# A layer of linear attention and a gated GLU: its side tasks dealt anew over two stages, and the scratch of the wo splits moved to other slots

## The chip, the cores and the metric

The kernel runs on one core of a Trainium2 chip. Its time is the device time of one execution in microseconds (us). Below, PE is TensorE (matmuls), DVE is VectorE, ACT is ScalarE, POOL is GpSimd, and SP is SyncE, whose queue issues nearly all DMAs.

## What is computed

With x of 2048 tokens by 1024 features and xn = layernorm(x), all in fp32:

```python
# 32 heads of 32 features; q, k, v = split(xn @ wqkv)
phi(a) = concat(softmax(a @ w_phi), softmax(-(a @ w_phi)))
num = phi(q) @ (phi(k).T @ v)                # per head, over all tokens
den = phi(q) @ sum(phi(k)) + 1e-6
s   = (num / den) @ wo
g   = silu((sigmoid(xn @ w_gate) * (xn @ w_up)) @ w_down)   # inner width 3584
out = x + s * g
```

## The kernel before

**Products.** Every large product of 2x2 blocks is made of seven block products and sums of blocks in place of eight (Strassen's scheme in Winograd's form). The seven are named B11, T2, T3, B21, T1, T4 and B22; they need sums of the blocks of both operands, and their results are combined as they leave PSUM. Each fp32 operand block is split into a high and a low fp32r part (`split`, L126: a cast on ACT at L128, a subtraction on DVE at L129), and each block matmul is three matmuls, high by high, high by low, low by high (`mm3`, L133 to L135).

**Stages.** The tokens go in two chunks, c = 0 and 1. For each chunk there is a projection stage (V, then K, then Q, each with seven products of 4 x 4 `mm3` in the order B11, B21, T2, T3, T4, T1, B22) and a GLU stage (28 units, gate and up in turn, of seven products of four `mm3`, in the order B11, T2, B21, T3, T1, T4, B22). So a GLU stage has 196 products, numbered by `m` in the code. Then come the down product for both chunks, and last the attention's numerators with the product by wo. The list `ops` holds all projection and GLU products; one loop (L803 on) emits them, each followed by `prep()`, which fills eight weight slots (28 to 35) ahead. In the first GLU stage all seven weight operands of a unit are split on the spot and the four that are sums are also stored to `ws_d`; in the second these four are loaded from there (L372).

**Slots.** On-chip memory is cut into 55 slots of 128 x 1024 fp32, grouped in blocks: x0 to x6 (0 to 27, the x operands, four slots each), w (28 to 35), p (36 to 38), fa (39 to 42), fb (43 to 46) and fc (47 to 54). The profile names the block, not the slot.

**Side tasks.** Other work of the layer is cut into tasks, which `background` (L797) takes from a queue, one at a given product:

- k tasks (`k_task`, L447), one a token tile and half of the heads: load k and v, softmax features on DVE and ACT, a running sum, two splits into 36 to 38, and eight matmuls (`kv_products`, L470) that the next call of `background` emits. They use 52, 53 and 54 too. After each half come `kv_sum`, `kv_blocks` and `z_broadcast`, which use PSUM banks 4 to 7 and the same slots.
- x tasks (`x_fetch` and `x_turn`, L522 and L529): load a tile of chunk 1's tokens, norm it, turn it, and store its x operands to `xo_d`; slots 52 to 54.
- q tasks (`q_features`, L598): the features of q; slots 36 to 38 for the first chunk, 43 and 44 for the second.
- o tasks (`o_task`, L257): load four blocks of wo into slots 52 and 53, make four sums on POOL (L269 to L272), split all seven operands through 36 to 38 in turn, and store them to `wo_d`, which the last stage reads.
- wd tasks (`wd_sums`, L558): load four blocks of w_down, make four sums on POOL, and store them to `wd_d`, for the down product's T2 and later; slots 47 and 52 for the first `WD1` of the 14, slots 43 and 44 for the others.

`tc.issue_after(anchor)` around a task lets its instructions be placed only behind the anchor, the last evacuation on DVE. Within that, the framework orders each engine's queue by its own simulated timeline; a slot that is used again makes the later user wait.

**Who runs where, before.** Beside the first Q projection, the k tasks of five tiles (behind T2, T3, T4, T1 and B22). In the first GLU stage 41 places: behind T2 of each unit from the second on, and behind T4 in units 0 to 13, so two a unit up to unit 13 and one a unit from there. They take the other three k tasks, then x and q tasks in turn (16 of each), then the four o tasks. In the second chunk's projections, eight wd tasks and five k tasks; in the second GLU stage 47 tasks, one at every fourth product: k tasks, six wd tasks and 16 q tasks, merged by the share of each that is left.

**The end of the first GLU stage.** In its last unit `load_operand` (L207) brings the second chunk's x operands from `xo_d`, in halves: half 0 through slot 53, half 1 through slot 54, each split into the x slots as soon as the last product that reads those is done. The V projection of chunk 1 follows at once.

Of the kernel before, what the change touches and what calls it, by code (L numbers as in the profile page):

```python
# [29 lines left out]
Q, K, V = 0, 1, 2  # L30
# [14 lines left out]
B11, T2, T3, B21, T1, T4, B22 = range(7)  # L45
# [3 lines left out]
def hedgehog_glu_kernel(  # L49
# [55 lines left out]
    block("fb", 43, 4, F32)  # L105
    block("fc", 47, 8, F32)
    NW = 8
    WD1 = 8

    banks = [psum.tile([P, HB], F32, name=f"bank{i}") for i in range(8)]  # L110

# [3 lines left out]
    def halves(*ids):  # L115
        return [slots[i][:, a] for i in ids for a in range(2)]

    def run(i, n):

        name, k = where[i]  # L120
        return blocks[name][0][:, k:k + n]
# [4 lines left out]
    def split(o, src):  # L126

        nc.scalar.copy(o[0], src)  # L128
        return nc.vector.tensor_sub(o[1], src, o[0].bitcast(F32))  # L129
# [127 lines left out]
    def o_task(k):  # L257

        def keep(i, b):
            o = slots[o_r.next()]  # L260
            split((o[:, 0].bitcast(F32R), o[:, 1].bitcast(F32R)), b)
            nc.sync.dma_start(wo_d[i, k], o.bitcast(F32).rearrange("p a n -> p (a n)"))

        a11, a12, a21, a22 = bs = halves(52, 53)
        for b, (f, h) in zip(bs, ((0, 0), (0, 1), (1, 0), (1, 1))):
            nc.sync.dma_start(b, wo[(k + 4 * h) * P:(k + 4 * h + 1) * P, f * HB:(f + 1) * HB])
        for i, b in ((B11, a11), (B21, a12), (T4, a22)):
            keep(i, b)
        nc.gpsimd.tensor_add(a22, a21, a22)  # L269
        nc.gpsimd.tensor_sub(a21, a11, a21)  # L270
        nc.gpsimd.tensor_sub(a11, a22, a11)
        nc.gpsimd.tensor_sub(a12, a12, a11)  # L272
        for i, b in ((T2, a11), (T3, a21), (T1, a22), (B22, a12)):
            keep(i, b)
# [109 lines left out]
    last_evac = []  # L384
# [173 lines left out]
    def wd_sums(j, *at):  # L558
        b11, b12, b21, b22 = b = halves(*at)
        for b, i in ((b11, B11), (b12, None), (b21, B21), (b22, B22)):  # L560
            nc.sync.dma_start(b, wd_block(i, j))
        sub = nc.gpsimd.tensor_sub
        sub(b11, b12, b11)
        sub(b12, b22, b12)
        sub(b22, b22, b11)
        sub(b21, b21, b22)
        for i, b in ((T1, b11), (T3, b12), (T2, b22), (T4, b21)):
            nc.sync.dma_start(wd_d[i, j], b)
# [29 lines left out]
    def q_features(t, hb):  # L598

        r, a, e = qf[t // CTT].next()  # L600
        p, e = slots[r][:, a], whole(e)
        nc.sync.dma_start(p, qkv_d[Q, t, hb])
        r = features(f"q{t}{hb}", p, e, True)
        nc.sync.dma_start(r_d[t, hb], r)
        nc.sync.dma_start(e_d[t, hb], e)
# [175 lines left out]
    qs = [lambda t=t, hb=hb: q_features(t, hb) for t in range(TT) for hb in range(2)]  # L781
    wd = [lambda j=j: wd_sums(j, *((47, 52) if j < WD1 else (43, 44))) for j in range(NJ)]
    xs = []
# [4 lines left out]
    bg_proj0 = deque(ks[0][:CTT])  # L788
    bg_glu0 = deque([lambda: block("p", 36, 3, F32)])
    for n in range(16):  # L790
        bg_glu0.extend([xs[n], qs[n]])
    bg_glu0.extend([lambda k=k: o_task(k) for k in range(4)])
    bg_proj1 = deque(wd[:WD1])
    late_k = deque(ks[0][CTT:] + ks[1])
    bg_glu1 = deque()

    def background(anchor, tasks):  # L797
        kv_products()
        if tasks:
            with tc.issue_after(anchor):  # L800
                tasks.popleft()()

    for n, (kind, c, what, i) in enumerate(ops):  # L803
        ws = ready[n]
        if kind == "proj":
            for u in range(4):
                if i in opening:
                    pbank[u] = pmm.next()
                xo = run(XO[i], 4)
                us = slice(u * P, (u + 1) * P)  # L810
                for k in range(4):
                    mm3(pbank[u], (xo[:, k, 0, us], xo[:, k, 1, us]), pair(ws[k]),
                        i in opening and k == 0, k == 3, skip_group_check=True)
                step()
            flow["used"] += 4
            while prep():
                pass
            for u in range(4):
                proj_out(c, what, i, u, pbank[u])
            if c == 0 and what == Q and i == B21:  # L820
                block("p", 36, 3, F32R)
            if c == 0 and what == Q and i not in (B11, B21):
                background(last_evac[0], bg_proj0)
            if c and not (what == V and i in (B11, B21)):
                background(last_evac[0], bg_proj1 if bg_proj1 else late_k if what == Q and i not in (B11, B21) else ())
            continue

        j, s = what
        u = units.index((c, j, s))
        if (j, s, i) == (0, 0, 0):  # L830
            step(1000)
        if i in opening:
            gbank[i] = gmm.next()
        bank = gbank[{B21: B11, T4: T3, B22: T1}.get(i, i)]
        w = [h.rearrange("p (k m) -> p k m", m=P) for h in pair(ws[0])]
        xo = run(XO[i], 4)
        for k in range(4):
            mm3(bank, (w[0][:, k], w[1][:, k]), (xo[:, k, 0], xo[:, k, 1]),
                i in opening and k == 0, k == 3, skip_group_check=True)
        flow["used"] += 1  # L840
        while prep():
            pass
        last_unit = u == len(units) - 1
        if flow["item"] == len(items) and flow["made"] - flow["used"] < NW:
            hfree.append(ws[0])
            if last_unit and i == 0:
                wfree.extend(range(16, 20))
            while wfree and down_prep():
                pass
        if i == B11:  # L850
            u1, u2 = ur.next(), ur.next()
            if s == 0:
                gates = [gates_r.next() for _ in range(4)]
            nc.scalar.copy(u1, bank)
        elif i == T2:
            v = nc.vector.tensor_add(u1, u1, bank)
        elif i == T3:
            v = nc.vector.tensor_add(u2, u1, bank)  # L858
        else:
            q = {B21: 0, T1: 3, T4: 2, B22: 1}[i]  # L860
            g = gates[q]
            if s == 0:
                if q == 0:
                    nc.scalar.activation(g, bank, AF.Sigmoid)
                else:
                    v = nc.vector.tensor_add(g, u2 if q == 3 else u1, bank)
                    nc.scalar.activation(g, g, AF.Sigmoid)
            else:
                if q == 0:
                    nc.vector.tensor_mul(g, g, bank)  # L870
                else:
                    b = u1 if q == 1 else u2
                    v = nc.vector.tensor_add(b, u2 if q == 3 else u1, bank)  # L873
                    nc.gpsimd.tensor_mul(g, g, b)  # L874
                if q != 1:
                    nc.sync.dma_start(h_d[(B11, None, B21, T4)[q], j, :, c], g)
                else:

                    a11, a21, a12, a22 = gates
                    s3, s2, s4 = [hs_r.next() for _ in range(3)]  # L880
                    nc.gpsimd.tensor_sub(s3, a11, a21)
                    nc.gpsimd.tensor_add(a21, a21, a22)
                    nc.gpsimd.tensor_sub(s2, a21, a11)
                    nc.gpsimd.tensor_sub(s4, a12, s2)
                    for o, b in ((T3, s3), (T1, a21), (T2, s2), (B22, s4)):
                        nc.sync.dma_start(h_d[o, j, :, c], b)

        m = (u % (2 * NJ)) * 7 + glu_order.index(i)
        if c == 0:
            if i == T2 and m > 7 or i == T4 and u < 14:  # L890
                background(v.ins, bg_proj0 or bg_glu0)
        else:
            if m == 0:
                rest = [deque(a) for a in (late_k, wd[WD1:], qs[16:])]
                total = [len(a) for a in rest]
                while any(rest):
                    q = max(range(3), key=lambda q: len(rest[q]) / total[q])
                    bg_glu1.append(rest[q].popleft())
            if m and m % 4 == 0:
                background(v.ins, bg_glu1)  # L900
        if c == 0 and u % (2 * NJ) == 2 * NJ - 1:
            if i == B11:
                load_operand(B11)
            elif i == B21:
                load_operand(B21)
            elif i == B22:
                for o in order[2:]:
                    load_operand(o)
                block("p", 36, 3, F32R)
# [114 lines left out]
    for tp_ in range(NTP):  # L1024
        nxt = attend(tp_ + 1) if tp_ + 1 < NTP else []
        n = 0
# [63 lines left out]
```

## Time and profile before

| | |
|---|---|
| median of 3 runs | 2440.74 us (2434.90 to 2442.89) |
| the profiled execution | 2439.86 us, its span 2438.0 us |
| granted TensorE clock, mean | 0.991 |
| moved by DMA | 626.17 MB, mean 257 GB/s |
| first GLU stage | from 302.5 to 866.7 us of the span |
| second GLU stage | from 1118.7 to about 1672 us |
| down product | from about 1672 us |

The profile is of one execution. A row of groups has: line, engine, operation, what it writes and reads with shapes, count | busy us, mean ns of one | idle time of the engine before it, and what ended that. A row of waits has: who waited for whom, us in total, times, the longest. A row of stretches has: the stretch, its length, then for each engine busy us and, in brackets, the number of instructions; then the granted clock, DMA's share and GB/s. A row of a timeline has: start, duration, engine, line, operation, and in square brackets the idle time before it and what ended it. A matmul's duration includes its way through the array, so the pace of TensorE is read from start to start.

### The profile page before, as it was taken

What the parts mean: (1) busy time and instruction counts of PE and PEld (TensorE: products, weight loads), DVE (VectorE), ACT (ScalarE), POOL (GpSimd) and SP (SyncE); (2) the same over time, 40 slices, a digit from 0 to 9 for tenths busy, and PEclk for the clock granted to TensorE, in tenths of its full rate; (3) what the DMA queues carried; (4) which work ended last, traced back from release to release, by engine and by line L of the source; (5) the groups of instructions that cost most, each with busy time, mean ns of one, the idle gap of its engine ahead of it and who ended that gap; (6) DMA issues with size and microseconds to landing.
All of it is one profiled execution on the core that took longest, in us unless ns stands there. A gap on an engine that the chain in (4) does not pass through costs nothing.

```text
span 2438.0 us, 31721 instructions
## 1 busy us (share of the span) xinstructions
PE 2360.2 (97%) x10728; PEld 1951.7 (80%) x10728; DVE 1786.3 (73%) x2341; ACT 996.5 (41%) x1485; POOL 1006.2 (41%) x638
## 2 busy tenths in 40 slices
PE   6999998999999969999999999999999999999998
PEld 5888876888888858888887888888888888788887
DVE  7533798888777856459758888875778786667885
ACT  6432355545444433234434434444333333345442
POOL 4530154676667743201334332333333334422655
PEclk9999999999999989999999999999999999999999
DMA  7874457999878999747787778779668766878664
GB/s 274 270 260 164 158 199 243 334 324 317 289 262 304 360 327 345 246 154 254 248 285 255 240 257 284 247 247 362 217 210 267 245 212 224 279 243 285 214 212 156
DMA packets 262323, 626.17 MB, mean 257 GB/s; under 512 B 37904, under 2 KB 58384, under 8 KB 257552
## 3 DMA queue, kind: packets, MB, share of 16 engines
q1 hardware_dynamic: 262160, 624.15, 75.1%
q8 instruction: 84, 1.38, 0.2%
q14 instruction: 79, 0.65, 0.1%
HBM read 374.47 MB, written 249.56 MB: 256 GB/s over the span
## 4 chain that ended last, share of the span: by engine, by line
PE 68%; DVE 13%; DMA 8%; issue 5%; POOL 3%; ACT 2%; SPq 1%; POOLq 0%; DVEq 0%; ACTq 0%
PE bank L133 22%; PE bank L135 22%; PE bank L134 22%; DVE w L129 3%; DVE x L129 1%; DMA fa<-w_down 1%; DVE p L129 1%; PE bank L475 1%; DMA fc<-xo_d 1%; DVE fc L452 1%; DMA f_d<-fc 1%; DMA fc<-qkv_d 0%; POOL fb L874 0%; DVE fc L435 0%; DMA w<-ws_d 0%
## 5 line engine op out<-in xcount | busy, mean ns | idle before, releaser
L133 PE MATMUL bank<-x,w 128*128 128x512 f32 x2352 | 912.2, 391 | 19.3 <-DVE fc L858 5.1
L134 PE MATMUL bank<-x,w 128*128 128x512 f32 x2352 | 918.0, 390 | 0.1
L135 PE MATMUL bank<-x,w 128*128 128x512 f32 x2352 | 907.7, 390 | 1.0 <-DVE w L129 1.0
L129 DVE TENSOR_TENSOR w<-fa,w 128x512 fp32r<-128x512 f32 (+1 forms) x444 | 447.7, 1012 | 213.5 <-ACT w L128 208.6
L133 PEld LDWEIGHTS bank<-x,w 128*128 128x128 f32 x2352 | 442.7, 188 | 120.3 <-DVE fc L858 8.2
L128 ACT CAST w<-fa 128x512 fp32r<-128x512 f32 (+1 forms) x444 | 308.4, 698 | 532.7 <-PE bank L134 385.9
L135 PEld LDWEIGHTS bank<-x,w 128*128 128x128 f32 x2352 | 442.8, 188 | 93.4 <-DVE w L129 1.4
L134 PEld LDWEIGHTS bank<-x,w 128*128 128x128 f32 x2352 | 442.9, 188 | 91.4 <-DVE x L129 1.0
L133 PE MATMUL bank<-w,x 128*128 128x512 f32 x708 | 279.5, 396 | 22.2 <-ACT x L128 19.8
L135 PE MATMUL bank<-w,x 128*128 128x512 f32 x708 | 278.5, 395 | 5.2 <-DVE x L129 5.1
L134 PE MATMUL bank<-w,x 128*128 128x512 f32 x708 | 279.0, 394 | 0.0
L874 POOL TENSOR_TENSOR fb<-fb,fc 128x512 f32<-128x512 f32 x57 | 90.5, 1588 | 219.5 <-DVE fc L873 202.7
L133 PEld LDWEIGHTS bank<-w,x 128*128 128x128 f32 x708 | 134.6, 190 | 52.2 <-ACT x L128 21.5
L613 POOL TENSOR_TENSOR fc<-fc 128x1024 f32<-128x1024 f32 x32 | 81.4, 2543 | 229.3 <-DMA fc<-e_d 120.4
L135 PEld LDWEIGHTS bank<-w,x 128*128 128x128 f32 x708 | 134.5, 190 | 35.0 <-DVE x L129 7.2
L134 PEld LDWEIGHTS bank<-w,x 128*128 128x128 f32 x708 | 134.6, 190 | 26.7
L129 DVE TENSOR_TENSOR x<-fa,x 128x512 fp32r<-128x512 f32 x112 | 117.1, 1046 | 33.8 <-ACT x L128 33.8
L334 POOL TENSOR_TENSOR fb<-fa 128x512 f32<-128x512 f32 x28 | 40.7, 1455 | 224.1 <-DMA fa<-w_gu 134.6
L129 DVE TENSOR_TENSOR w<-fb,w 128x512 fp32r<-128x512 f32 (+1 forms) x114 | 116.2, 1020 | 14.7 <-ACT w L128 14.6
L128 ACT CAST p<-fc 128x512 fp32r<-128x512 f32 x100 | 74.9, 756 | 124.6 <-DVE fc L452 77.8
L129 DVE TENSOR_TENSOR p<-fc,p 128x512 fp32r<-128x512 f32 x100 | 112.0, 1127 | 16.8 <-ACT p L128 16.7
L128 ACT CAST w<-fb 128x512 fp32r<-128x512 f32 (+1 forms) x114 | 70.7, 623 | 85.1 <-PE bank L134 70.7
(239 smaller groups left out, 3188.6 us busy)
## 6 DMA issues: line engine op xcount, KB each, us to landing
ws_d<-w SPq DMA_DIRECT2D x112, 512.0 KB, 4.6
w<-ws_d SPq DMA_DIRECT2D x112, 512.0 KB, 5.1
fa<-w_gu SPq DMA_DIRECT2D x84, 512.0 KB, 4.9
fa<-h_d SPq DMA_DIRECT2D x84, 512.0 KB, 4.7
fa<-wf_d SPq DMA_DIRECT2D x32, 1024.0 KB, 6.4
h_d<-fc SPq DMA_DIRECT2D x120, 256.0 KB, 4.4
h_d<-fb SPq DMA_DIRECT2D x76, 256.0 KB, 4.8
fc<-qkv_d SPq DMA_DIRECT2D x64, 256.0 KB, 3.6
```

The source lines that it names most:

```text
L128: nc.scalar.copy(o[0], src)
L129: return nc.vector.tensor_sub(o[1], src, o[0].bitcast(F32))
L133: nc.tensor.matmul(o, a[0], b[0], start=first, stop=False, **kw)
L134: nc.tensor.matmul(o, a[0], b[1], start=False, stop=False, **kw)
L135: nc.tensor.matmul(o, a[1], b[0], start=False, stop=last, **kw)
L334: nc.gpsimd.tensor_add(s1, a21, a22)
L452: nc.vector.tensor_mul(e3, e3, r[:, :, None].to_broadcast([P, 32, DH]))
L475: nc.tensor.matmul(kvb[g // 2][:, g % 2 * 256:g % 2 * 256 + 256], v[:, g].rearrange("p a f -> p (a f)"), ph[:, g].rearrange("p a f -> p (a ...
L613: nc.gpsimd.tensor_mul(ez, e, zb)
L874: nc.gpsimd.tensor_mul(g, g, b)
```

## The change

The four o tasks leave the first GLU stage and are put at the head of the wd tasks in the second one; their four blocks are held in slots 43 and 44 instead of 52 and 53. `WD1` goes from 8 to 6, so two wd tasks more come in the second GLU stage. Beside the first Q projection four k tasks are started instead of five, behind B11, T2, T4 and B22. In the first GLU stage the four k tasks that are left, a change of the p block, four x tasks, then x and q tasks in turn, and four q tasks, 37 in all, are put at products 7 to 185 at even spacing. In the second, 53 tasks are put at products 3 to 187 at even spacing, where there were 47 at every fourth product.

```diff
--- before.py
+++ after.py
@@ -105,7 +105,7 @@
     block("fb", 43, 4, F32)
     block("fc", 47, 8, F32)
     NW = 8
-    WD1 = 8
+    WD1 = 6
 
     banks = [psum.tile([P, HB], F32, name=f"bank{i}") for i in range(8)]
 
@@ -261,7 +261,7 @@
             split((o[:, 0].bitcast(F32R), o[:, 1].bitcast(F32R)), b)
             nc.sync.dma_start(wo_d[i, k], o.bitcast(F32).rearrange("p a n -> p (a n)"))
 
-        a11, a12, a21, a22 = bs = halves(52, 53)
+        a11, a12, a21, a22 = bs = halves(43, 44)
         for b, (f, h) in zip(bs, ((0, 0), (0, 1), (1, 0), (1, 1))):
             nc.sync.dma_start(b, wo[(k + 4 * h) * P:(k + 4 * h + 1) * P, f * HB:(f + 1) * HB])
         for i, b in ((B11, a11), (B21, a12), (T4, a22)):
@@ -788,8 +788,9 @@
     bg_proj0 = deque(ks[0][:CTT])
     bg_glu0 = deque([lambda: block("p", 36, 3, F32)])
     for n in range(16):
-        bg_glu0.extend([xs[n], qs[n]])
-    bg_glu0.extend([lambda k=k: o_task(k) for k in range(4)])
+        bg_glu0.extend([xs[n]] if n < 4 else [xs[n], qs[n - 4]])
+    bg_glu0.extend(qs[12:16])
+    os = [lambda k=k: o_task(k) for k in range(4)]
     bg_proj1 = deque(wd[:WD1])
     late_k = deque(ks[0][CTT:] + ks[1])
     bg_glu1 = deque()
@@ -817,10 +818,10 @@
                 pass
             for u in range(4):
                 proj_out(c, what, i, u, pbank[u])
-            if c == 0 and what == Q and i == B21:
+            if c == 0 and what == Q and i == B11:
                 block("p", 36, 3, F32R)
-            if c == 0 and what == Q and i not in (B11, B21):
-                background(last_evac[0], bg_proj0)
+            if c == 0 and what == Q:
+                background(last_evac[0], bg_proj0 if i in (B11, T2, T4, B22) else ())
             if c and not (what == V and i in (B11, B21)):
                 background(last_evac[0], bg_proj1 if bg_proj1 else late_k if what == Q and i not in (B11, B21) else ())
             continue
@@ -887,16 +888,21 @@
 
         m = (u % (2 * NJ)) * 7 + glu_order.index(i)
         if c == 0:
-            if i == T2 and m > 7 or i == T4 and u < 14:
-                background(v.ins, bg_proj0 or bg_glu0)
+            if m == 0:
+                bg_glu0.extendleft(reversed(bg_proj0))
+                bg_proj0.clear()
+                due = [7 + n * 178 // (len(bg_glu0) - 1) for n in range(len(bg_glu0))]
+            if m in due:
+                background(v.ins, bg_glu0)
         else:
             if m == 0:
-                rest = [deque(a) for a in (late_k, wd[WD1:], qs[16:])]
+                rest = [deque(a) for a in (late_k, os + wd[WD1:], qs[16:])]
                 total = [len(a) for a in rest]
                 while any(rest):
                     q = max(range(3), key=lambda q: len(rest[q]) / total[q])
                     bg_glu1.append(rest[q].popleft())
-            if m and m % 4 == 0:
+                due = [3 + n * 188 // len(bg_glu1) for n in range(len(bg_glu1) + 1)]
+            if m in due:
                 background(v.ins, bg_glu1)
         if c == 0 and u % (2 * NJ) == 2 * NJ - 1:
             if i == B11:
```

## The prediction

> **What bounds the kernel now.** I read the page first, for the engine that sets the time.
>
> ```profile
> span 2438.0 us, 31721 instructions
> PE 2360.2 (97%) x10728; PEld 1951.7 (80%) x10728; DVE 1786.3 (73%) x2341; ACT 996.5 (41%) x1485; POOL 1006.2 (41%) x638
> ```
>
> TensorE is busy 97% of the span, so only its gaps can be won. Next I cut the span at the stages and asked for the busy time of each stretch.
>
> ```profile
> core 0: us, PE busy (x) PEld busy (x) DVE busy (x) ACT busy (x) POOL busy (x), PEclk, DMA share, GB/s
> 227.00:302.50 75.50, 75.50 (x343) 62.80 (x342) 48.75 (x60) 25.40 (x31) 7.99 (x5) 1.00 0.46 153
> 302.50:392.00 89.50, 81.10 (x354) 64.65 (x353) 84.39 (x100) 44.83 (x64) 39.64 (x22) 0.96 0.59 207
> 392.00:502.00 110.00, 104.81 (x450) 83.93 (x449) 97.99 (x141) 55.34 (x77) 70.22 (x48) 0.98 0.90 316
> 502.00:780.00 278.00, 277.05 (x1221) 228.54 (x1220) 220.64 (x307) 132.00 (x194) 178.40 (x120) 1.00 0.84 294
> 780.00:866.70 86.70, 86.70 (x383) 71.35 (x382) 76.86 (x75) 36.56 (x61) 62.11 (x40) 1.00 0.98 359
> 866.70:910.00 43.30, 24.25 (x97) 18.95 (x96) 18.53 (x17) 16.17 (x22) 20.63 (x14) 0.80 0.92 315
> 1118.70:1257.00 138.30, 138.30 (x637) 115.35 (x636) 106.17 (x144) 62.10 (x85) 45.32 (x32) 1.00 0.81 276
> 1257.00:1396.00 139.00, 135.21 (x607) 112.06 (x607) 106.82 (x139) 57.02 (x76) 42.07 (x27) 0.99 0.74 244
> 1396.00:1672.00 276.00, 274.57 (x1254) 228.18 (x1253) 228.45 (x284) 120.36 (x163) 93.88 (x63) 1.00 0.78 267
> 1672.00:1800.00 128.00, 128.00 (x567) 106.01 (x566) 87.96 (x118) 46.13 (x81) 46.59 (x22) 1.00 0.75 256
> ```
>
> The first row is the last 75 us of the Q projection of chunk 0; 302.5 to 866.7 is the first GLU stage, 866.7 begins the second chunk's projections, 1118.7 to 1672 is the second GLU stage. The undisturbed pace is 277.05/1221 = 0.227 us a matmul, so a product of 12 takes 2.72 us. What each stretch loses against that pace, slow clock included: 302.5 to 392 has 354 matmuls, 48 of them the narrow ones of six k tasks (8 each, counted half, an estimate): 306 x 0.227 + 48 x 0.113 = 74.9, so 14.6 us lost. 392 to 502: 450 x 0.227 = 102.2, 7.8 lost. 502 to 780: 1.0. 780 to 866.7: nothing. 866.7 to 910: 97 x 0.227 = 22.0, 21.3 lost. Second GLU stage, by idle time: 0 + 3.8 + 1.4 = 5.2. That is 49.9 us in all that this change can reach.
>
> The largest loss is one gap, which the timeline of TensorE shows, then those of SyncE, GpSimd and ScalarE:
>
> ```profile
> 877.35 0.39 PE L135 MATMUL bank<-w,x 128*128 128x512 f32 x1
> 895.73 0.80 PE L133 MATMUL bank<-w,x 128*128 128x512 f32 x1 [17.99 <-ACT x L128]
> ```
> ```profile
> 861.33 0.44 SPq L266 DMA_DIRECT2D fc<-wo  x1
> ...
> 885.91 2.43 SPq L211 DMA_DIRECT2D fc<-xo_d  x2
> ```
> ```profile
> 881.22 1.27 POOL L272 TENSOR_TENSOR fc<-fc 128x512 f32<-128x512 f32 x1
> ```
> ```profile
> 894.63 1.04 ACT L128 CAST x<-fc 128x1024 fp32r<-128x1024 f32 x1 [6.45 <-DMA fc<-xo_d]
> ```
>
> Slots 52 and 53 hold the four blocks of an o task; load_operand stages half 0 of every x operand in 53. The last o task still loads wo at 861.33, its GpSimd sums end at 882.5, and only then, at 885.91, is x loaded into 53; its split begins when that lands at 894.6, and the product follows at 895.73. So the chain is slot 53, not bandwidth: the o task ahead of the load in the slot's order.
>
> The second loss is VectorE's. TensorE's waits inside the first GLU stage are led by an evacuation:
>
> ```profile
> PE bank L133 <- DVE fc L858: 5.1, 6, 2.3
> ```
>
> VectorE is busy 84.39 of 89.5 us there (94%), because six k tasks run in it, one every (390.4 - 305.4)/5 = 17 us:
>
> ```profile
> L463 DVE TENSOR_TENSOR fc<-fc x6: 1211/1212/1715, 305.4 to 390.4; 128x1024 f32<-128x1024 f32 x6
> ```
>
> **The change, part by part.** Prices of VectorE in the first GLU stage, first by operation, then all the work of a q task (tile stq) and most of a k task's (tile stk; this view names the first GLU stage, then the second):
>
> ```profile
> L129 DVE TENSOR_TENSOR w<-fb,w 128x512 fp32r<-128x512 f32 x110 | 110.3, 1003 | 14.7 <-ACT w L128 14.6
> L129 DVE TENSOR_TENSOR w<-fa,w 128x512 fp32r<-128x512 f32 x82 | 85.0, 1036 | 6.3 <-ACT w L128 6.3
> L129 DVE TENSOR_TENSOR p<-fc,p 128x512 fp32r<-128x512 f32 x28 | 31.7, 1146 | 6.1 <-ACT p L128 6.1
> L873 DVE TENSOR_TENSOR fc<-fc,bank 128x512 f32<-128x512 f32 x41 | 27.7, 676 | 16.4 <-PE bank L135 10.3 <-POOL fb L874 4.7 <-POOL fc L874 1.2
> ```
> ```profile
> 302.50:866.70 564.20, 87.89 (x96) 0.99 0.83 294
> ```
> ```profile
> 302.50:866.70 564.20, 32.13 (x35) 0.99 0.83 294
> 1118.70:1672.00 553.30, 126.59 (x145) 1.00 0.77 264
> ```
>
> The stage's own work: 7 splits a unit at 1.0 and 5.5 evacuations at 0.68, 10.7 us in 19.05 us, or 1.53 a product. A q task is 87.89/16 = 5.5 us. A k task is 126.59/20.7 = 6.1 (145 operations, 7 a task), plus zacc 1.2, the value split 1.15 and the wide split about 1.4 (twice a 0.68 operation): 9.9. An x task is 1.4 (four 0.68 operations for two tasks; the norm's one-column ones left out). An o task is 7 splits: 8.0.
>
> *k tasks earlier and fewer in Q.* Five in the last five Q products become four, one each second product. The Q stretch loses nothing today with VectorE at 48.75 of 75.5, and one task fewer is 9.9 less: no gain, no cost. Today six k tasks run beside the first GLU stage; after, the one behind B22 and four more at products 7, 11, 16, 21. One k task of 17 us meets 6.2 products of own work (9.6) and 9.9 of its own plus a wait on its exponential: over 17 either way, so beside k tasks VectorE stays too full. Five for six, the first with more room: 14.6 becomes 9.5 (between 3, if lag drains in the 4.9 products between tasks, and 15). **-5.**
>
> *x first, then x and q evenly.* 37 tasks at 178/36 = 4.94 products instead of two a unit up to unit 13. A pair then has 26.9 us for 15.1 + 5.5 + 1.4 = 22.0, 82%; today it has 19.05 for 10.7 + 6.9, 92%. The nearest rows: 220.64/278 (79%) lost 1.0 us, 76.86/86.7 (89%) nothing. So 7.8 becomes 0.8. **-7** (-4 to -8). The four q tasks left to the end have 13.4 us each for 7.6 + 5.5, 98%, where today nothing is lost: **+0.5** (0 to 5).
>
> *o tasks out of the first GLU stage.* Slot 53's last user before load_operand is then the last x turn, at product 160 of 196, some 98 us before the stage ends; both halves of B11 can wait in 53 and 54. What is late next is the following half through the two slots, for which the view of that line has the landing:
>
> ```profile
> DMA to landing us min/median/max: 4.8/5.8/8.7
> ```
>
> 5.8 us of load and some 3 of split (1.04 on ScalarE by the cast above, two 1.0 operations' worth on VectorE): about 9 us an operand with two slots, against 4 x 4 x 3 x 0.227 = 10.9 us a projection product, and B11 and B21 have their x slots free 7 and 5 products before the stage's end. It keeps pace. 21.3 becomes 2, for a short wait or two. **-19.3** (-10 to -21).
>
> *o tasks and two more wd tasks in the second GLU stage*, one task each 3.55 products instead of 4. The row of GpSimd for an o task:
>
> ```profile
> L269 POOL TENSOR_TENSOR fc<-fc x4: 1684/1792/2272, 779.4 to 875.1; 128x512 f32<-128x512 f32 x4
> ```
>
> The merge puts the four o tasks at products 6, 24, 38 and 52. VectorE gains 32 us and GpSimd 16 x 1.7 = 27, nearly all by 1280. Three of them bring the first 138 us to 106.17 + 24 = 130, 94%. Bounds: the 94% of 302.5 to 392 lost 14.6/89.5, or 16%, which is 22 us; the 89% of 780 to 866.7, with o tasks themselves in it, lost nothing. I take **+6**, nearer the latter: it is the same task. Two wd tasks move into the stage with no VectorE work; their 8 sums and 16 DMAs leave the second chunk's projections, for which I count no gain, and take 43 and 44: nothing, unless the slots jam, below. The o tasks' 44 DMAs pass SyncE's queue, and their 4 x (1.0 + 3.6) = 18.4 MB come to 114 GB/s over 161 us, less some 25 for two wd tasks that leave that part: 276 + 89 = 365 GB/s, where 359 is the most that a row above shows. What the products wait for is
>
> ```profile
> w<-ws_d SPq DMA_DIRECT2D x112, 512.0 KB, 5.1
> ```
>
> and eight w slots leave it 7 products or 19 us; 359 GB/s beside the first stage's own loads cost nothing. Taken at 0, inside the 6.
>
> Sum: -5 - 7 + 0.5 - 19.3 + 6 = -24.8. The profiled execution took 2439.86 (1.9 around its span), the median of the runs 0.9 more: 2440.7 - 24.8 = **2416**.
>
> **Two rules beside the rows.** After a short wait the clock is halved here:
>
> ```profile
> 367.99 0.79 PE L133 MATMUL bank<-x,w 128*128 128x512 f32 x1 [2.32 <-DVE fc L858]
> ...
> 369.01 0.63 PE L135 MATMUL bank<-x,w 128*128 128x512 f32 x1
> 369.44 0.63 PE L133 MATMUL bank<-x,w 128*128 128x512 f32 x1
> ```
>
> 0.43 us apart instead of 0.227, after 2.32 us of idling. The Trainium skill (TensorE: Matmul & The Clock Gate, Part 1: The HAM clock gate) has the clock fall only after an idle window of about 3.4 us; by that rule the k part's remaining waits would cost themselves alone, an estimate of 7 rather than 9.5, and the time would be some 2.5 us lower. I stay with the row.
>
> The other one speaks against the change. Splits of one shape differ by what runs beside them:
>
> ```profile
> L129 DVE TENSOR_TENSOR p<-fc,p x19: 679/1774/1784, 783.5 to 866.3; 128x512 fp32r<-128x512 f32 x19
> ```
> ```profile
> L129 DVE TENSOR_TENSOR w<-fa,w x22: 678/683/1779, 1120.4 to 1256.6; 128x512 fp32r<-128x512 f32 x22
> ```
>
> The median is 1.77 where GpSimd is busy 62.11 of 86.7 us and 0.68 where it is 45.32 of 138.3. The Trainium skill (GPSIMD Engine Reference, 1. Specifications) says that GpSimd's way to SBUF is shared with VectorE and contended by instructions with two SBUF inputs; the rows agree.
>
> **The rivals.** *VectorE fills up beside the o tasks (0.14).* By those rows 27 us of GpSimd stretch 27 x (1 - 0.68/1.77) = 17 us of VectorE work. Then the first 138 us are full, and lose the 16%: 22 for 6. Time 2432, near the line of no change; with the four late q tasks at their 5, 2436.
>
> *Part of the gap stays (0.18).* If the halves come through 53 and 54 more slowly than 10.9 us an operand, or the late q tasks hold back their splits, half the gap is left: +9, 2425. For it: one of these loads took 8.7 us, and DMA stands at 0.92 to 0.98 there. Against it: 9 us an operand is under 10.9, with both halves of the first waiting.
>
> *Slower: slots 36 to 38 jam (0.11).* An o task and a k task both need them.
>
> ```profile
> L262 SPq DMA_DIRECT2D wo_d<-p x28: 319/324/1732, 778.1 to 888.9; - x28
> ```
> ```profile
> L519 ACT COPY fc<-bank x4: 587/589/590, 1267.7 to 1681.1; 128x512 f32<-128x512 f32 x4
> ```
>
> Four o tasks held them from 778 to some 894, 29 us each. Up to product 56 the second GLU stage has 53 x 2.82 = 150 us for 4 x 29 + 4 k tasks x 17 = 184, 34 late; fifteen later k tasks come every 20.1 us and take 17, which regains 47. So they end in time, 13 us to spare. At 44 us an o task they end 47 late. z_broadcast, which now ends at 1681.7 without a loss (128.00 of 128.00), would hold the banks of the down products' second chunk until 1729: 45 us of waiting, 2440.7 - 31 + 6 + 45 = 2461. The point is an o task of about 40 us. Against it: a k task needs these slots only for its last operations. Slots 43 and 44, which q, wd and o tasks share, will run late as well, but what comes of them is wanted late: the first wd sums only at T2, 14 steps of 24 matmuls or 76 us into the down product.
>
> **How the numbers follow.** Forecast 0.57 (2403 to 2424); part of the gap 0.18; full VectorE 0.14, of which 0.10 within 0.3%; jam 0.11. 0.3% is 7.3 us, about what a measurement of this kernel can tell from no change. Faster 0.79, same 0.10, slower 0.11. The low end takes the k part's 3, the gap's -21 and nothing in the second GLU stage: 2440.7 - 11.6 - 8 - 21 = 2400. The high end is the full VectorE with late q tasks, 2437; above it lies the jam.
>
> **What would show it.** Right: no TensorE wait over 3 us between 850 and 910; L211's first two loads 90 us ahead of the stage's end; L858 waits fewer after 392; wo_d stores from 1130 to 1300, with VectorE over 85% there. Wrong: a gap after the second GLU stage with L519 later than 1690, or PE idle over 15 us between 1100 and 1260.

## The result, and the profile after

The changed kernel takes 2423.14 us (median of 5 runs, 2418.18 to 2425.68), the kernel before 2440.69 us beside it (5 runs). The ratio is 0.993, 95% interval 0.9909 to 0.995: about 17 us or 0.7% faster. The profiled execution of after is the slowest of its five, 2425.68 us with a span of 2423.9, 14.1 us under the span of before. All stretches below are of that execution, and its stages come earlier as it goes on: the first GLU stage ends at 854.7 us (866.7 before), the second begins at 1084.4 (1118.7).

The stretches of the kernel after, up to the start of the second chunk's projections, with the columns of the prediction:

```profile
302.50:392.00 89.50, 85.40 (x380) 70.44 (x379) 84.79 (x101) 42.95 (x61) 43.91 (x25) 0.96 0.62 228
392.00:502.00 110.00, 108.13 (x473) 88.86 (x472) 81.80 (x117) 50.20 (x74) 68.42 (x48) 0.98 0.86 286
502.00:780.00 278.00, 276.88 (x1222) 228.93 (x1221) 217.70 (x304) 130.27 (x187) 177.80 (x123) 1.00 0.82 287
780.00:854.70 74.70, 74.70 (x332) 61.84 (x331) 59.28 (x76) 33.77 (x48) 33.56 (x23) 1.00 0.75 273
854.70:910.00 55.30, 55.30 (x246) 45.79 (x245) 37.45 (x33) 25.46 (x29) 27.07 (x18) 1.00 0.94 332
```

The last row is the place of the 18 us gap: TensorE is busy 55.30 of 55.30 us at full clock. From 302.5 to 392 it now does 380 matmuls where it did 354, from 392 to 502 it does 473 instead of 450. VectorE's share from 392 to 502 has gone from 89% to 74%.

The second GLU stage went the other way. A good ruler for it is the copy that opens each of its 28 units (line 854 before, 855 after): the time from the first to the last of them is 27 units. The rows of that line, before and then after:

```profile
L854 ACT COPY fc<-bank x28: 562/580/590, 1121.6 to 1670.6; 128x512 f32<-128x512 f32 x28
```
```profile
L855 ACT COPY fc<-bank x28: 565/581/590, 1087.3 to 1658.6; 128x512 f32<-128x512 f32 x28
```

549.0 us before, 571.3 after: 22.3 us lost. By the same ruler the first GLU stage went from 543.7 us (307.5 to 851.2) to 535.4 (307.0 to 842.4). The whole second stage, before and then after:

```profile
1118.70:1685.00 566.30, 561.09 (x2553) 466.33 (x2552) 448.97 (x578) 244.45 (x330) 184.28 (x123) 1.00 0.78 267
```
```profile
1084.40:1671.80 587.40, 567.86 (x2553) 467.30 (x2551) 468.73 (x605) 259.40 (x358) 223.28 (x147) 0.99 0.85 296
```

The first row ends at 1685, where the last product of the stage is done; the prediction had taken its end at 1672. The same 2553 matmuls take 21.1 us more: TensorE's idle time went from 5.2 to 19.5 us, and its busy time grew by 6.8 us at a clock of 0.99 instead of 1.00. VectorE's share is 79% before and 80% after, so its sum of work over the stage does not explain the loss. The longest groups of TensorE's waits are these:

```profile
PE bank L133 <- DVE fc L859: 4.5, 3, 3.1
PE bank L475 <- DVE p L129: 4.1, 2, 3.3
PE bank L133 <- DVE fb L867: 3.6, 3, 2.8
PE bank L133 <- ACT fc L855: 3.1, 3, 2.5
```

They are few and long, and 13 of the 19.5 us are behind VectorE: it was not short of time on average, but late at some places.

### The profile page after: what moved, and what is told of

Read it like the earlier page. It is cut to its first block, busy times and chain, and to the rows that moved or that the text cites. A ratio compares the mean times of both kernels' runs of the same rounds, so it can differ in the third digit from the quotient of the medians.

```text
span 2423.9 us, 31722 instructions
## 1 busy us (share of the span) xinstructions
PE 2359.0 (97%) x10728; PEld 1952.8 (81%) x10728; DVE 1760.6 (73%) x2341; ACT 996.8 (41%) x1484; POOL 1001.3 (41%) x638
## 5 line engine op out<-in xcount | busy, mean ns | idle before, releaser
L129 DVE TENSOR_TENSOR w<-fa,w 128x512 fp32r<-128x512 f32 (+1 forms) x444 | 442.4, 1000 | 215.1 <-ACT w L128 197.1
L875 POOL TENSOR_TENSOR fb<-fb,fc 128x512 f32<-128x512 f32 x57 | 90.8, 1592 | 203.1 <-DVE fc L874 203.1
L875 POOL TENSOR_TENSOR fc<-fc 128x512 f32<-128x512 f32 x27 | 41.0, 1518 | 230.1 <-ACT w L128 172.4
L128 ACT CAST x<-fa 128x512 fp32r<-128x512 f32 x112 | 69.4, 620 | 75.7 <-DMA fa<-wd_d 38.9
```

## The experiments

Two theories stood at first for the second GLU stage: (A) the o tasks hold slots 36 to 38 and make the k tasks late; (B) the two wd tasks more, with their sums on GpSimd, and the denser dealing. Each kernel below was timed beside the kernel before on its own chip. "First copies" is the ruler above, of one profile each. The times of one kernel lie up to 10 us apart from run to run, and the profiled execution of after is the slowest of its five, so a difference of a few us between two rulers says little by itself.

**o_dma_only.** The o tasks of the changed kernel without their sums and splits:

```python
# the whole body of o_task
        for b, (f, h) in zip(halves(43, 44), ((0, 0), (0, 1), (1, 0), (1, 1))):
            nc.sync.dma_start(b, wo[(k + 4 * h) * P:(k + 4 * h + 1) * P, f * HB:(f + 1) * HB])
        for i in (B11, B21, T4, T2, T3, T1, B22):
            nc.sync.dma_start(wo_d[i, k], whole(43 + i % 2))
```

> The changed kernel, whose o tasks keep their 44 DMAs and their hold on slots 43 and 44 but leave out the sums and splits (raw blocks of wo are stored), so they no longer use slots 36 to 38, VectorE, ScalarE or GpSimd. In the changed kernel the first copies of the 28 units of the second GLU stage lie 571.3 us apart from first to last, before 549.0. Theory A (the o tasks' part on slots 36 to 38 and on VectorE makes the k tasks late, which then bunch and fill VectorE): that distance falls to 547 to 556 and the time to 2400 to 2409. Rival B (two more wd tasks, their sums on GpSimd, and the denser dealing, whatever the o tasks do): the distance stays at 564 or more, the time at 2416 or more.

```profile
L843 ACT COPY fc<-bank x28: 564/578/589, 1087.0 to 1646.8; 128x512 f32<-128x512 f32 x28
```

559.8 us; 2415.8 us, ratio 0.9907 (0.9886 to 0.9928). It falls between the two: 11.5 of the 22.3 us are gone with the o tasks' work, 10.8 stay without it. Neither theory holds alone.

**wd8.** The changed kernel with

```diff
-    WD1 = 6
+    WD1 = 8
```

> The changed kernel with WD1 back at 8: six wd tasks instead of eight in the second GLU stage, 51 tasks instead of 53. Theory A (o tasks make k tasks late): the distance of first copies in the second GLU stage stays within 5 us of 571.3 and the time at 2418 to 2427. Rival B (wd sums on GpSimd stretch VectorE's operations, and the dealing is too dense): a third or more of the 22 us comes back, distance 555 to 564, time 2405 to 2415.

```profile
L855 ACT COPY fc<-bank x28: 565/577/590, 1088.2 to 1644.6; 128x512 f32<-128x512 f32 x28
```

556.4 us, ratio 0.9887 (0.9869 to 0.9906), 2410.6 us. Two of 53 tasks account for 14.9 of the 22.3 us by the ruler, and for 12.6 us by the medians (10.5 by the ratios); both are inside what B expected. All four o tasks are still in the stage. The 11.5 us that go with the o tasks' work and the 14.9 that go with two wd tasks add up to more than 22.3, so the two parts make each other worse.

**o_only.** The kernel before with the o tasks alone moved:

```diff
-        a11, a12, a21, a22 = bs = halves(52, 53)
+        a11, a12, a21, a22 = bs = halves(43, 44)
...
-    bg_glu0.extend([lambda k=k: o_task(k) for k in range(4)])
+    os = [lambda k=k: o_task(k) for k in range(4)]
...
-                rest = [deque(a) for a in (late_k, wd[WD1:], qs[16:])]
+                rest = [deque(a) for a in (late_k, os + wd[WD1:], qs[16:])]
...
-            if m and m % 4 == 0:
+            if m in [3 + n * 188 // 51 for n in range(52)]:
```

> The kernel before with one part of the change alone: the four o tasks go from the first GLU stage to the head of the wd tasks of the second, in slots 43 and 44, with 51 tasks dealt evenly there; the first GLU stage keeps its dealing. The gap's theory (slot 53, held by the last o task): TensorE has no wait over 3 us between 850 and 910, which is worth 20 us; the second GLU stage loses 15 to 22 as in the changed kernel; time 2434 to 2442, about that of before. If the gap came from the dealing in the first GLU stage instead, 8 us or more of it stay and the time is above 2445.

The stretch of the gap, and the ruler of the second stage:

```profile
866.70:910.00 43.30, 43.30 (x193) 35.85 (x192) 32.81 (x25) 22.43 (x26) 24.34 (x14) 1.00 0.94 336
```
```profile
L854 ACT COPY fc<-bank x28: 566/579/590, 1097.9 to 1655.6; 128x512 f32<-128x512 f32 x28
```

The gap is gone (43.30 of 43.30), with the old dealing. The expected time was missed on the good side: 2419.0 us, ratio 0.9927 (0.9909 to 0.9945), as fast as the whole change. The second stage takes 557.7, so the four o tasks with six wd tasks cost it 8.7 us, not 15 to 22.

**dealt_o_stays.** The dealing alone; the o tasks stay in the first GLU stage:

```diff
-        a11, a12, a21, a22 = bs = halves(43, 44)
+        a11, a12, a21, a22 = bs = halves(52, 53)
...
-    WD1 = 6
+    WD1 = 8
...
-    os = [lambda k=k: o_task(k) for k in range(4)]
+    bg_glu0.extend([lambda k=k: o_task(k) for k in range(4)])
...
-                rest = [deque(a) for a in (late_k, os + wd[WD1:], qs[16:])]
+                rest = [deque(a) for a in (late_k, wd[WD1:], qs[16:])]
```

> The other part alone: the new dealing of the first Q projection and of the first GLU stage, but with the o tasks at its end in slots 52 and 53, 41 tasks in all, and the second GLU stage with 47 tasks evenly dealt. The gap's theory: the wait for slot 53 stays, 10 to 25 us between 840 and 910, whatever the spacing; the first GLU stage gains its 8 to 13 us; the second one is as before, 547 to 553 between first copies. Time 2424 to 2434. If even spacing is what removes the gap: no wait over 3 us there, time 2403 to 2412.

```profile
906.58 0.79 PE L133 MATMUL bank<-w,x 128*128 128x512 f32 x1 [32.09 <-ACT x L128]
```

The gap is there, with the same releaser, and longer than I had expected (10 to 25 us): the last sum of the last o task starts 36 us behind the stage's end (894.1 against 858.4), where before it was 15 (881.2 against 866.7). Time 2450.5 us, not 2424 to 2434; ratio 1.004 (1.0025 to 1.0055). One of its seven executions took 12892 us, which no trace explains; it is not in the ratio. First copies take 535.4 us in the first GLU stage (307.2 to 842.6), the same as in the changed kernel, and 550.2 in the second. So the dealing gives its 8.3 us in the first stage and costs the second about 1 (550.2 against 549.0). It does not remove the gap, and with the o tasks left in the first stage it makes it longer.

**wd_no_sums.** A second round asked what of a wd task costs. The changed kernel, without the sums of its wd tasks in the second GLU stage:

```diff
-        sub(b11, b12, b11)
-        sub(b12, b22, b12)
-        sub(b22, b22, b11)
-        sub(b21, b21, b22)
+        if j < WD1:
+            sub(b11, b12, b11)
+            sub(b12, b22, b12)
+            sub(b22, b22, b11)
+            sub(b21, b21, b22)
```

> The changed kernel, whose eight wd tasks of the second GLU stage leave out their four sums on GpSimd (raw blocks of w_down are stored); loads, stores and the hold on slots 43 and 44 stay. From the first four runs: six wd tasks in place of eight took 16 us off the second GLU stage. Theory C (the sums on GpSimd: they stretch VectorE's two-input operations, and gate products queue behind them): the distance of first copies in the second GLU stage falls from 571.3 to 552 to 560, time 2403 to 2412. Rival D (slots 43 and 44: wd tasks hold them and make q tasks late): nothing much changes, 565 or more, time 2416 or more.

Its ruler, and the whole stage:

```profile
L856 ACT COPY fc<-bank x28: 566/579/589, 1087.7 to 1642.1; 128x512 f32<-128x512 f32 x28
```
```profile
1084.80:1655.90 571.10, 561.96 (x2552) 465.91 (x2551) 456.76 (x605) 260.51 (x358) 177.35 (x115) 1.00 0.87 305
```

554.4 us, 16.9 less; 2407.3 us, ratio 0.9872 (0.9855 to 0.9889). The eight wd tasks still load and store through 43 and 44, DMA still moves as much, the 53 places are the same, and yet most of the loss is gone. So it is the sums on GpSimd, not the denser dealing. (Without the sums a store need not wait for them, so 43 and 44 come free a little earlier as well; this run does not separate the two.) The sums do two things. 223.28 - 177.35 = 45.9 us less of GpSimd work made VectorE's 605 instructions 12.0 us shorter (468.73 to 456.76). And a sum that waits for its load holds up what is queued behind it.

Counting TensorE's wide matmuls (those of 512 columns) from the stage's start finds the places. Up to the 1008th the two kernels are level (243.9 us and 244.6). Between the 1008th and the 1680th, and again between the 2016th and the 2184th, they part; in each pair the first row is the changed kernel, the second wd_no_sums:

```profile
1328.30:1505.90 177.60, 166.21 (x746) 136.25 (x745) 161.89 (x196) 75.40 (x96) 80.76 (x49) 0.98 0.83 284
1329.40:1496.80 167.40, 162.38 (x746) 134.37 (x745) 150.94 (x196) 76.22 (x96) 48.69 (x29) 1.00 0.89 309
```
```profile
1586.90:1632.60 45.70, 41.61 (x186) 32.88 (x185) 29.14 (x42) 18.36 (x29) 22.84 (x19) 1.00 0.80 269
1576.90:1616.90 40.00, 40.00 (x185) 33.16 (x184) 28.49 (x43) 18.37 (x29) 13.32 (x11) 1.00 0.88 296
```

The first place costs 10.2 us. VectorE is busy 91% of it, and its 196 instructions take 10.9 us longer than the 196 of wd_no_sums. The second place costs 5.7 us, and VectorE's work there is hardly longer: it is held up. Against wd8 the same two places cost 11.8 and 5.7 of 16.2 us. The second place begins with this, first on GpSimd and then on VectorE:

```profile
1576.42 1.29 POOL L563 TENSOR_TENSOR fb<-fb 128x512 f32<-128x512 f32 x1 [15.87 <-DMA fb<-w_down]
1586.04 1.29 POOL L564 TENSOR_TENSOR fb<-fb 128x512 f32<-128x512 f32 x1 [8.33 <-DMA fb<-w_down]
1587.41 1.29 POOL L565 TENSOR_TENSOR fb<-fb 128x512 f32<-128x512 f32 x1
1588.77 1.29 POOL L566 TENSOR_TENSOR fb<-fb 128x512 f32<-128x512 f32 x1
1590.02 1.29 POOL L875 TENSOR_TENSOR fb<-fb,fc 128x512 f32<-128x512 f32 x1
```
```profile
1591.34 0.69 DVE L874 TENSOR_TENSOR fc<-fc,bank 128x512 f32<-128x512 f32 x1 [7.98 <-POOL fb L875]
```

L875 is a gate product of the GLU. It needs no w_down, but it stands behind L564, which waited 8.33 us for a block of w_down; VectorE, which must not overwrite what L875 reads, then stood for 7.98 us in front of an evacuation. TensorE did not lose all of that: its waits from there to 1632.6 are short and come to 4.1 us. An example of the first place is at 1346 us, rows of VectorE, GpSimd and TensorE:

```profile
1342.75 1.77 DVE L434 TENSOR_TENSOR fc<-fc,stk 128x512 f32<-128x512 f32 x1
1344.44 1.75 DVE L435 TENSOR_TENSOR fc<-stk,fc 128x512 f32<-128x512 f32 x1
1346.11 0.67 DVE L859 TENSOR_TENSOR fc<-fc,bank 128x512 f32<-128x512 f32 x1
```
```profile
1340.65 1.62 POOL L566 TENSOR_TENSOR fb<-fb 128x512 f32<-128x512 f32 x1
1342.24 1.73 POOL L875 TENSOR_TENSOR fc<-fc 128x512 f32<-128x512 f32 x1
1344.05 1.59 POOL L882 TENSOR_TENSOR fc<-fc 128x512 f32<-128x512 f32 x1
1345.72 1.61 POOL L883 TENSOR_TENSOR fc<-fc,fb 128x512 f32<-128x512 f32 x1
```
```profile
1346.84 0.80 PE L133 MATMUL bank<-x,w 128*128 128x512 f32 x1 [3.15 <-DVE fc L859]
```

The wd sums have run straight into the gate sums of the unit, GpSimd has no pause, and a k task's two subtractions take 1.77 and 1.75 us each where the shortest in the stage takes 0.68; the evacuation L859 behind them is late by what TensorE then waits.

**o_spread.** The changed kernel, its o tasks spread among the wd tasks:

```diff
-                rest = [deque(a) for a in (late_k, os + wd[WD1:], qs[16:])]
+                rest = [deque(a) for a in (late_k, [f for n in range(4) for f in (wd[WD1 + 2 * n], os[n], wd[WD1 + 2 * n + 1])], qs[16:])]
```

> The changed kernel with the four o tasks spread among the eight wd tasks of the second GLU stage (wd, o, wd four times over) instead of all ahead of them. If it is the backlog behind four o tasks in a row that bunches later tasks: the distance falls from 571.3 to 556 to 563 and the time to 2406 to 2414. If it is the amount of GpSimd and VectorE work in the stage: within 5 us of 571.3, time 2417 to 2427.

```profile
L855 ACT COPY fc<-bank x28: 564/578/590, 1086.6 to 1648.1; 128x512 f32<-128x512 f32 x28
```

561.5 us, 9.8 less with every operation the same; 2415.8 us, ratio 0.9908 (0.9891 to 0.9925), 2 us above the range of the first theory. So where the tasks stand counts, beside how much they are.

**wd7 and wd4.** Seven and ten wd tasks in the second GLU stage (`WD1 = 7`, `WD1 = 4`).

> The changed kernel with WD1 = 7: seven wd tasks in the second GLU stage, 52 tasks. With eight the first copies of the stage lie 571.3 us apart, with six 556.4. If every wd task there costs its 7 us: 561 to 567, time 2413 to 2420. If the cost is a matter of which sums happen to stand ahead of a gate product in GpSimd's queue, and not of their number: anywhere from 552 to 575, and the run with ten tells more.

> The changed kernel with WD1 = 4: ten wd tasks in the second GLU stage, 55 tasks. If every wd task there costs some 7 us: 580 to 592 between first copies, time 2430 to 2443. If slots 43 and 44 are full at eight already: more, and q and wd tasks end in the down product. If only the accident of the order counts: 575 or less, time 2427 or less.

The rulers, of wd7 and then of wd4:

```profile
L855 ACT COPY fc<-bank x28: 565/581/592, 1084.9 to 1649.2; 128x512 f32<-128x512 f32 x28
```
```profile
L855 ACT COPY fc<-bank x28: 565/579/601, 1087.1 to 1661.8; 128x512 f32<-128x512 f32 x28
```

With six, seven, eight and ten wd tasks: 556.4, 564.3, 571.3 and 574.7 us. Seven is in the range of "each costs its 7 us" (2418.3 us, ratio 0.9917, 0.9902 to 0.9931), ten is not: two more add 3.4, with 2426.8 us, ratio 0.9947 (0.993 to 0.9964). Ten lies just inside what was expected if only the order counts (575 and 2427 or less). So the time grows with the number in all four runs, but not in proportion, and the place in the order has a part that these runs do not separate. Slots 43 and 44 did not run over: the last store of a wd task goes out at 1630.4 us in wd4, before the stage ends.

**o_proj1, wd14 and wd8_spread** are versions that the runs point to. The first takes the o tasks into the second chunk's V and K projections:

```diff
-        a11, a12, a21, a22 = bs = halves(43, 44)
+        a11, a12, a21, a22 = bs = halves(53, 54)
...
-    WD1 = 6
+    WD1 = 8
...
-    bg_proj1 = deque(wd[:WD1])
+    bg_proj1 = deque(wd[:3] + [f for n in range(4) for f in (os[n], wd[3 + n])] + wd[7:WD1])
...
-                rest = [deque(a) for a in (late_k, os + wd[WD1:], qs[16:])]
+                rest = [deque(a) for a in (late_k, wd[WD1:], qs[16:])]
```

> A version that the runs so far point to: the changed kernel with WD1 = 8 and the o tasks in the second chunk's V and K projections, one behind every other wd task, blocks in slots 53 and 54 (free once the x operands are loaded). The second GLU stage then has 47 tasks evenly dealt. Theory: it goes back to 547 to 553 between first copies, the projections lose nothing or up to 4 us, no gap at their start; time 2402 to 2409. If o tasks cost as much beside a projection: 2412 or more.

2408.3 us, ratio 0.9878 (0.9861 to 0.9894), first copies 553.9 us (1087.7 to 1641.6), 5 more than before and 1 more than expected. The second, all wd tasks into those projections (`WD1 = 14`):

> The changed kernel with all 14 wd tasks in the second chunk's projections (WD1 = 14), so that the second GLU stage has 45 tasks: k, q and the four o tasks, and no wd sums. Theory C (wd sums on GpSimd cost the time there, o tasks little): 549 to 556 between first copies, time 2402 to 2409, if the projections and the k tasks behind them take the eight tasks more at no loss. Rival (the o tasks are what costs): 563 or more, time 2414 or more.

2428.1 us, ratio 0.9962 (0.9946 to 0.9977), first copies 557.8 us (1103.4 to 1661.2), in neither range, the time 14 us above the rival's lower bound, and a wait that no theory had, on TensorE:

```profile
1064.85 0.79 PE L133 MATMUL bank<-w,x 128*128 128x512 f32 x1 [11.34 <-DVE fc L395]
```

SyncE and VectorE tell it:

```profile
1051.29 7.25 SPq L568 DMA_DIRECT2D wd_d<-fc  x4
1058.78 0.32 SPq L449 DMA_DIRECT2D fc<-qkv_d  x1
```
```profile
1062.18 0.69 DVE L129 TENSOR_TENSOR p<-fc,p 128x512 fp32r<-128x512 f32 x1 [14.10 <-ACT p L128]
...
1064.11 0.68 DVE L395 TENSOR_TENSOR fc<-fc,bank 128x512 f32<-128x512 f32 x1
```

The last wd task and the first k task share slot 52. The load of the k task's v goes out at 1058.78, behind the wd task's four stores; the split of v waits 14.10 us at the head of VectorE's queue, and the projection's evacuation L395 stands behind it. Again a task that is late by its slot, and a queue in a fixed order. The second GLU stage of wd14 has no wd sums at all and is 1.4 us from that of wd8, which has six. So six cost nothing there that this ruler shows; the loss comes with the seventh and eighth.

The third has `WD1 = 8` and the o tasks spread among four of the six wd tasks.

> The changed kernel with WD1 = 8 and the four o tasks spread among the first of the six wd tasks of the second GLU stage. Spreading gained 9.8 us of first copies beside eight wd tasks. If the backlog behind four o tasks in a row is what is left of the stage's loss (556.4 against 549.0 before): 549 to 553, time 2402 to 2407. If spreading helps only because eight wd tasks jam: 554 to 559, time 2408 to 2413.

2408.2 us, ratio 0.9876 (0.9861 to 0.9892), first copies 554.0 us (1086.9 to 1640.9): 2.4 less than wd8, at the lower end of the second range in both numbers, and not to be told from wd8 in time. So spreading the o tasks brings little where there are six wd tasks. These three, wd8, o_proj1 and wd8_spread, beat both kernels; the intervals do not order them.

**x_not_first.** The changed kernel without its x tasks ahead:

```diff
-        bg_glu0.extend([xs[n]] if n < 4 else [xs[n], qs[n - 4]])
-    bg_glu0.extend(qs[12:16])
+        bg_glu0.extend([xs[n], qs[n]])
```

> The changed kernel without its x tasks first: in the first GLU stage x and q tasks in turn from the start, 37 tasks at the same even spacing. If even spacing makes the first stage's gain (VectorE under 90% behind the k tasks): its 551 us stay within 3 us and the time at 2418 to 2428. If the x tasks ahead give VectorE the time to catch up behind the k tasks: 4 to 8 us more in the stretch after 392, time 2427 to 2432.

2417.7 us, ratio 0.991 (0.9894 to 0.9927), first copies of the first GLU stage 534.4 us (307.5 to 841.9) against 535.4. So the x tasks ahead bring nothing; the even spacing, with the new places of the k tasks, does it. Which of these two does more was not tested.

## Why the prediction was right, and where it was off

- *The gap (predicted -19.3).* Right in place and cause. 866.7 to 910 lost 21.3 us before; nothing is lost there after. o_only removes it with the old dealing, dealt_o_stays brings it back with the new one, and what differs at that place is the o tasks in slots 52 and 53. The short wait or two that I had left in (2 us) did not come. The first two loads of x through slots 53 and 54 went out at 775.4 and 777.4 us, 79 and 77 us ahead of the stage's end, not 90; it was early enough.
- *The first GLU stage (predicted -5, -7, +0.5).* About right in sum, with the parts shifted. The prediction counted 48 narrow matmuls from 302.5 to 392; the trace before has 40 there and 8 just behind, so the losses before were 13.7 and 8.8 us, not 14.6 and 7.8. After, 34 of 380 are narrow: 346 x 0.227 + 34 x 0.113 = 82.4 us of work in 89.5, so 7.1 lost: -6.6 for -5. From 392 to 502 it is 465 x 0.227 + 8 x 0.113 = 106.5 of 110, 3.5 lost: -5.3 for -7. The four q tasks at the end lost nothing: 74.70 of 74.70. By its ends the stage went from 564.2 us (302.5 to 866.7) to 551.3 (303.4 to 854.7); the ruler of first copies, which leaves out the ends, shows 8.3 of these 12.9 us.
- *The o tasks in the second GLU stage (predicted +6).* About right: 8.7 us in o_only, 7.4 in wd8. The place is right too (stores from 1125.5 to 1306.7 us), but VectorE was not over 85% busy there, as I had said it would be: it was 82% busy in the first 138 us of the stage and 71% where the stores are.

```profile
1084.40:1222.40 138.00, 135.23 (x614) 111.86 (x613) 112.50 (x152) 68.22 (x97) 44.50 (x31) 0.99 0.85 295
1125.00:1307.00 182.00, 179.23 (x797) 147.83 (x797) 130.07 (x174) 79.93 (x120) 77.63 (x53) 0.99 0.90 316
```

- *The two wd tasks: the step that failed.* "Two wd tasks move into the stage with no VectorE work": "nothing, unless the slots jam". Measured, they cost 14.9 us by the ruler (571.3 - 556.4), two thirds of the stage's loss, and 10.5 to 12.6 by the medians of the runs. I counted a task by its work on VectorE and by its slots and left out what its sums on GpSimd do to VectorE's operations and to GpSimd's queue. The prediction had rows for the first of these and used them for the o tasks' sums alone. The rival of a full VectorE had the size (22 us for 6), and the stretching that it named is there, but it put the loss beside the o tasks, in the first 138 us of the stage. Three of the four waits over 2 us came behind them, at 1347, 1399 and 1427 us: the first two beside wd and gate sums, the third behind a k task's split with no sum beside it.
- *The jam of slots 36 to 38* did not come: the last copy of z_broadcast starts at 1665.0 us, ahead of the stage's end at 1671.8.
- *Sum.* Of the two spans' difference of 14.1 us, the first stage gave -12.9 (forecast -11.5), the gap -21.3 (-19.3) and the second stage +21.1 (+6), which leaves -1.0 to the rest. The medians lie 17.5 apart; 24.8 was forecast. That the result came within 7 us of 2416 is in part luck: two gains larger than forecast hid 3.4 us of a cost that was 15 us larger. The median of 2423.1 stands 1 us inside the forecast's 2403 to 2424, and its interval (2418.5 to 2428.5) reaches past it.

That the sums cause most of the second stage's loss is shown by wd_no_sums. How it divides is read from one trace of each kernel: 10.2 us where VectorE's instructions are stretched, 5.7 where a gate product stands behind a sum that waits for its load. No run has one of the two without the other. What is left without the sums is 5.4 us by the ruler (554.4 against 549.0).

## What to carry to other kernels

Price a moved task on every engine that it touches. Sums on GpSimd made VectorE's work 10.9 us longer where VectorE was 91% busy, and one sum of 1.3 us that waited 8 us for its load held a gate product and VectorE behind it. Before spreading tasks by time, look at which scratch slot the next stage's first load needs, and who holds it last; one slot was worth 21 us here, the whole new dealing of the first stage 8 to 13. And split a change that gains and loses: the part that lost most was two tasks of 53, and without it the same change gives 0.9887 of the time before instead of 0.993.

## What I had not expected of the hardware

TensorE can run at half pace for a while after quite short waits. The wait of 3.15 us at 1346.84, quoted above, was followed by these rows:

```profile
1347.43 0.63 PE L134 MATMUL bank<-x,w 128*128 128x512 f32 x1
1347.86 0.63 PE L135 MATMUL bank<-x,w 128*128 128x512 f32 x1
1348.28 0.63 PE L133 MATMUL bank<-x,w 128*128 128x512 f32 x1
```

0.43 us apart instead of 0.227, as after the wait of 2.32 us in the prediction. The same came after a wait of 1.87 us:

```profile
465.48 0.50 PE L133 MATMUL bank<-x,w 128*128 128x512 f32 x1 [1.87 <-DVE fc L859]
...
466.49 0.63 PE L133 MATMUL bank<-x,w 128*128 128x512 f32 x1
466.92 0.63 PE L134 MATMUL bank<-x,w 128*128 128x512 f32 x1
```

After one of 2.83 us at 1399.42 and one of 1.05 us at 1605.12 the pace was the usual one. So a wait of 2 to 3 us can cost more than itself, and its length alone does not say whether it will; what else decides is open here. The Trainium skill (TensorE: Matmul & The Clock Gate, Part 1: The HAM clock gate) has the half rate after an idle window of about 3.4 us; these rows show it after less.
